# Alpha in 384 B rows, running sums in 64-row products, and more q, k turned by transfers, in a fused linear-attention and feed-forward kernel

## The chip, the cores and the metric

The kernel runs on one core of a Trainium2 chip. The metric is the device time of one execution in microseconds (us). The engines named are TensorE (PE, its weight loads PEld), VectorE (DVE), ScalarE (ACT), GpSimd (POOL) and SyncE (SP), which here only issues transfers (DMA).

## The reference

Attention with a decaying state, per batch and head, followed by a feed-forward stage on the same 3072 tokens of 384 features. B, H, S, D are 4, 8, 768, 48; d_ff is 768. All inputs and the output are float32.

```python
for t in range(S):
    state = alpha[:, :, t, :, None] * state + np.einsum('bhd,bhe->bhde', k[:, :, t], v[:, :, t])
    y[:, :, t] = np.einsum('bhd,bhde->bhe', q[:, :, t], state)
...
x = y.transpose(0, 2, 1, 3).reshape(B * S, H * D)
h = np.maximum(np.maximum(x @ w1, x @ w2), x @ w3)
out = h @ w_out
```

## The kernel before

The sequence is cut into 6 blocks of 128 tokens. A unit is one block of one batch with its 8 heads: 24 units, 0 to 23, batches inside blocks. Two units make a group, 12 in all. A group's alpha, q, k and v are loaded into tiles `an`, `qn`, `kn`, `vn` (five of each, in turn) with 128 tokens on the partitions and 16 heads of 48 float32 beside each other; a token's row of one head in DRAM is 192 B long. The first four groups are loaded by halves, one unit at a time, in an order written out by hand (`FIRST`), in which the pieces of the four weight matrices stand too ("w"; w1 is 0, w2 is 1, w3 is 2, w_out is 3, each cut after column 256 into piece 0 and piece 1).

Per group, ScalarE takes Ln of alpha into `la` (L538). Per unit, one product with a constant triangle (`tri`, L591, `cums`) gives the running sums of the logarithms, about the middle of the block. ScalarE makes exp of plus and minus that (`ep`, `en`, L594, L596). q times `ep` and k times `en` go to `qk` (L603, POOL or VectorE), v scaled to `v16` (L615 POOL, L610 ScalarE). Both q and k are then turned, so that features are on the partitions: by eight TensorE transposes and a VectorE copy (`turn_in`, L573, L577), or, for units in `CROSS_Q`, by one transfer from SP (`cross`, L622). Scores are eight products on 48 rows, in pairs on the upper and lower half of the array (L637); VectorE multiplies them with the causal mask into `LA` (L642); `LA` with v16, and the turned q with the state `Z`, give the output (L680, L683), which ScalarE scales into `xb` (L691). `xb` is turned into `xT` by three TensorE transposes and a copy (L705, L709) or, for units in `CROSS_X`, by a transfer (L697). The state of a block follows from the sums k times v (L735), VectorE (`U`, L741) and POOL (`Z`, L748), with factors `G` from the block's total decay (L551, L557, L563).

The feed-forward stage uses max(a, b, c) = a + relu(max(b - a, c - a)): `wd` holds w2 - w1 and w3 - w1 (L482, `subs`), and the term x @ w1 @ w_out is one product with `w1o`, made from w1 turned (L503, L509) and w_out (L520, `folded`). A feed-forward step (`ffn`) takes one unit (the first four) or two; per three or two columns blocks of 128 it multiplies with the w2 part (L776), ScalarE takes relu (L787), multiplies with the w3 part (L776), VectorE takes the maximum into `hT` (L792); then L810 multiplies with `w1o` and w_out, and the result leaves by ScalarE copies and transfers (L821, L829). w_out is loaded into the tile that w1 came in, once both pieces of w1 have been cast (L461).

The order of all instructions comes from a planner: each step has an engine, a cost in us, a rank, what it reads and writes, and the planner lists the steps of each engine by the time at which its own model has them ready; engines then work through their lists in order, and wait. `LEAD` ranks the feed-forward steps, `EARLY` names the engines of q, k, v work of some units, `SUBS` those of the differences, `PAIRS` the unit from which on two units' scores stand in one step. Loads keep the order of the program on SP; q, k transfers and xb transfers are put between them where the plan has them ready. `WARM` puts products with zeros (L717) on TensorE behind a unit's q or k product where the plan leaves TensorE free.

Of the kernel before, what the change touches and what calls it, by code (L numbers as in the profile page):

```python
# [10 lines left out]
FP32 = mybir.dt.float32  # L11
# [20 lines left out]
LEAD = (9.0, 7.5, 8.0, 9.0)  # L32
EARLY = {0: ("DVE", "DVE", "POOL"), 2: ("DVE", "POOL", "ACT"), 6: ("DVE", "POOL", "ACT"),
         8: ("DVE", "POOL", "ACT"), 11: ("POOL", "POOL", "ACT")}
WCUTS = (0, 256, 768)
SUBS = {(1, 0): "POOL", (1, 1): "DVE", (2, 0): "DVE", (2, 1): "POOL", (1, 2): "DVE",
        (2, 2): "POOL"}
FIRST = (("v", 1, 1, 2), ("va", 0, 1, 2), ("va", 0, 0, 1), ("k", 0, 1, 2), ("q", 1, 1, 2),
         ("a", 1, 0, 1), ("v", 1, 0, 1), ("k", 1, 0, 1), ("q", 1, 0, 1), ("k", 0, 0, 1),
         ("q", 0, 1, 2), ("w", 0, 0), ("a", 1, 1, 2), ("w", 0, 1), ("q", 0, 0, 1), ("w", 1, 1),  # L40
         ("k", 1, 1, 2), ("w", 3, 1), ("w", 3, 0), ("w", 1, 0), ("w", 2, 1), ("a", 2, 0, 1),
         ("w", 2, 0), ("k", 2, 0, 1), ("aq", 2, 1, 2), ("q", 2, 0, 1), ("q", 3, 0, 1),
         ("k", 2, 1, 2), ("a", 3, 0, 1), ("a", 3, 1, 2), ("v", 2, 0, 1), ("v", 2, 1, 2),
         ("k", 3, 0, 1), ("k", 3, 1, 2), ("q", 3, 1, 2), ("v", 3, 1, 2), ("v", 3, 0, 1))
WARM = (0, 1, 21)
WPOOL, ROWS, WTAX = {}, False, 0.1
SINGLE, LAST = 4, 0
PAIRS, WIDE = 10, 99
CROSS_Q = (18, 19, 20, 22, 23)
CROSS_X = (18, 19, 20, 21, 22, 23)  # L50
# [239 lines left out]
def kernel(  # L290
# [39 lines left out]
    halves = np.stack([rr < HALF, rr >= HALF], axis=1).astype(np.float32)  # L330
    c16_np = np.concatenate(
        [trimid, np.eye(P), (s_ <= t_).astype(np.float32), halves], axis=1
# [9 lines left out]
    c16 = sb.tile([P, 3 * P + 2], FP16, name="c16")  # L342
    c32 = sb.tile([P, 3], FP32, name="c32")
    tri, ident = c16[:, :P], c16[:, P:2 * P]
    maskA, hsel = c16[:, 2 * P:3 * P], c16[:, 3 * P:]
# [33 lines left out]
    w1o = sb.tile([P, NFT, DM], FP16, name="w1o")  # L379
    for t in las:  # L380
        nc.vector.memset(t[:, :, D:], 0.0)
    for t in qks:
        nc.vector.memset(t[:, :, :, D:], 0.0)
# [30 lines left out]
    def load(n, lo, hi, names="aqkv"):  # L414
        cb, g = divmod(n, B // UB)
        for x in names:
            t = ld[x][n % 5]

            def run(x=x, t=t):
                nc.sync.dma_start(  # L420
                    t[:, lo:hi],
                    views[x][cb * P:(cb + 1) * P, g * HG + lo:g * HG + hi])

            plan.step("SP", 0.5, -1.0, run, line="loads",
                      writes=[(x, n % 5, h) for h in range(lo // H, hi // H)],
                      load=1.80 * (hi - lo) / HG,
                      late=0.0 if n < 3 else SPARE)
            asked.append((x, n % 5, lo // H))
# [22 lines left out]
    def wload(g, part):  # L451
# [6 lines left out]
                  load=(3.15 if ROWS else 3.25) * size(part) / (NFT * DF) + WTAX)  # L458
# [19 lines left out]
    def subs(g, part):  # L478
# [7 lines left out]
                  reads=[("ws", g, part), ("w", 0, part)], writes=[("wd", g, part)])  # L486
# [44 lines left out]
    def decay(n):  # L531
        cb, g = divmod(n, B // UB)
        la, an = las[n % 3], ld["a"][n % 5]
        rank = 2 * n - 0.5

        def ln(lo, hi):
            plan.step("ACT", 0.2 + 0.00083 * (hi - lo) * D, rank,
                      lambda: nc.scalar.activation(out=la[:, lo:hi, :D], in_=an[:, lo:hi, :],  # L538
                                                   func=AFT.Ln, scale=1.0 / CDEC),
# [8 lines left out]
        def totals():  # L548
            live[key] = bank(key, [P, HG // 2, 2], FP32)
            for j in range(HG // 2):  # L550
                nc.tensor.matmul(live[key][:, j, :], la[:, 2 * j:2 * j + 2, :], hsel,  # L551
                                 start=True, stop=True)
# [14 lines left out]

    def turn_in(u, qk, qkT, tk):
        def trans():
            live[tk] = bank(tk, [P, 2, NP, P], FP16)  # L570
            for w in range(2):
                for j in range(NP):
# [3 lines left out]
                  reads=[("qk", u % 7, 0), ("qk", u % 7, 1)], writes=[tk, ("qkT room", u % 3)])  # L576
        plan.step("DVE", 0.69, u, lambda: nc.vector.tensor_copy(out=qkT, in_=live[tk]),  # L577
                  reads=[tk], writes=[("qkT", u % 3)])

    def prep(u):  # L580
# [3 lines left out]
        qk, v16 = qks[u % 7], v16s[u % 7]  # L584
        Lk, tk = ("Lp", u), ("tp", u)
        Ak = ("A", u)
        plan.width[Ak] = 2

        def cums():
            live[Lk] = bank(Lk, [P, H, D], FP32)  # L590
            nc.tensor.matmul(live[Lk], tri, la[:, hs, :D], start=True, stop=True)  # L591

        plan.step("PE", 0.162, u, cums, banks=[Lk], reads=[("la", n % 3, i)], writes=[Lk])
        plan.step("ACT", 0.49, u, lambda: nc.scalar.activation(out=ep, in_=live[Lk], func=AFT.Exp),  # L594
                  reads=[Lk], writes=[("ep", u % 3)])
        plan.step("ACT", 0.49, u, lambda: nc.scalar.activation(out=en, in_=live[Lk], func=AFT.Exp,  # L596
                                                               scale=-1.0),
                  reads=[Lk], writes=[("en", u % 3)])
        for w, x, e in ((0, "q", ep), (1, "k", en)):
            eng = EARLY[u][w] if u in EARLY else "POOL"  # L600
            plan.step(eng, 1.0 if eng == "POOL" else 0.56, u,
# [5 lines left out]
                      writes=[("qk", u % 7, w)])  # L607
# [11 lines left out]
        qkT, LA = qkTs[u % 3], LAs[u % 3]  # L619
# [5 lines left out]
        if u in CROSS_Q:  # L625
            plan.step("SP", 1.2, -2.0, cross, load=1.35, late=0.2,
                      reads=[("qk", u % 7, 0), ("qk", u % 7, 1)],
                      writes=[("qkT room", u % 3), ("qkT", u % 3)])
# [19 lines left out]
        if u < PAIRS:  # L648
            plan.step("PE", 0.23, u, scores, banks=[Ak], mode=1,
                      reads=[("qkT", u % 3), ("qkT room", u % 3)], writes=[Ak, ("LA room", u % 3)])  # L650
# [3 lines left out]
        else:  # L654
            first, made, v, Bk = held.pop()

            def both():
# [4 lines left out]
                      reads=[("qkT", x % 3) for x in (v, u)] + [("qkT room", x % 3) for x in (v, u)],  # L662
# [6 lines left out]
    def output(u):  # L669
        n, i = divmod(u, UB)  # L670
        cb, b = divmod(u, B)
        qkT, LA, v16, xb = qkTs[u % 3], LAs[u % 3], v16s[u % 7], xbs[u % 5]
# [262 lines left out]
```

## Time and profile before

| | |
|---|---|
| runs | 159.16, 157.71, 155.82 us; median 157.71 |
| profiled execution | 154.24 us, its span 152.5 us |
| TensorE busy | 133.9 us (88%), 1647 products |
| VectorE, ScalarE, POOL busy | 92.5, 87.2, 74.1 us |
| transfers | 30.58 MB, 114,211 packets, 107,792 of them under 512 B |
| SP's queue (q1) | 83.6% of 16 engines' span |
| granted TensorE clock | 0.996 of full |

The page cuts the span into 40 slices of 3.8 us and gives each engine's busy share of a slice in tenths, 9 for 90% or more; a busy TensorE can hold products that wait for nothing but their own pipeline. The chain of waits is followed back from the last instruction: at each step to what released it, or to the instruction ahead of it on its engine. In lists of instructions the bracket behind a line is the idle time of the engine before it and what ended it. The profiled execution is one execution on its own; the runs shown are others.

### The profile page before, as it was taken

What the parts mean: (1) busy time and instruction counts of PE and PEld (TensorE: products, weight loads), DVE (VectorE), ACT (ScalarE), POOL (GpSimd) and SP (SyncE); (2) the same over time, 40 slices, a digit from 0 to 9 for tenths busy, and PEclk for the clock granted to TensorE, in tenths of its full rate; (3) what the DMA queues carried; (4) which work ended last, traced back from release to release, by engine and by line L of the source; (5) the groups of instructions that cost most, each with busy time, mean ns of one, the idle gap of its engine ahead of it and who ended that gap; (6) DMA issues with size and microseconds to landing.
All of it is one profiled execution on the core that took longest, in us unless ns stands there. A gap on an engine that the chain in (4) does not pass through costs nothing.

```text
span 152.5 us, 4135 instructions
## 1 busy us (share of the span) xinstructions
PE 133.9 (88%) x1647; PEld 105.0 (69%) x1647; DVE 92.5 (61%) x159; ACT 87.2 (57%) x177; POOL 74.1 (49%) x101
## 2 busy tenths in 40 slices
PE   0133979999999999999999999999979999999990
PEld 0012567769789878698697888687867786868660
DVE  7004645837687998788595799484496583606030
ACT  3362476688367675687747667669419354543411
POOL 0423105184732619594987598598964880000000
PEclk9999999999999999999999999999999999999998
DMA  6999999989999989989899999989999976321113
GB/s 122 208 218 232 325 269 315 352 210 188 222 266 206 234 173 244 280 174 238 177 295 180 256 269 187 231 212 219 169 207 210 154 197 131 110 82 52 53 55 103
DMA packets 114211, 30.58 MB, mean 201 GB/s; under 512 B 107792, under 2 KB 113040, under 8 KB 114192
## 3 DMA queue, kind: packets, MB, share of 16 engines
q1 hardware_dynamic: 111744, 27.37, 83.6%
q10 hardware_dynamic: 2448, 2.95, 7.0%
q8 instruction: 13, 0.21, 0.5%
q14 instruction: 6, 0.05, 0.1%
HBM read 23.69 MB, written 4.72 MB: 186 GB/s over the span
## 4 chain that ended last, share of the span: by engine, by line
PE 76%; DMA 10%; SPq 8%; ACT 2%; issue 1%; POOL 1%; DVE 0%; ACTq 0%
PE psum L776 29%; PE psum L810 21%; SPq L420 7%; PE psum L573 5%; DMA ws<-in_moe_w_dram 4%; DMA qkT<-qk 4%; PE psum L637 4%; PE psum L683 3%; PE psum L591 2%; PE psum L680 2%; PE psum L705 2%; PE psum L717 2%; DMA xT<-xb 2%; PE psum L520 2%; PE psum L735 2%; PE psum L551 1%
## 5 line engine op out<-in xcount | busy, mean ns | idle before, releaser
L776 PE MATMUL psum<-xT,wd 128*128 128x256 f16 (+1 forms) x504 | 53.9, 257 | 0.3 <-DMA xT<-xb 0.2
L776 PEld LDWEIGHTS <-wd 128*128 128x128 f16 x504 | 42.0, 98 | 5.5 <-issue 0.5
L642 DVE TENSOR_TENSOR LA<-psum,c 128x1024 f16<-128x1024 f32 x24 | 28.6, 1220 | 9.7 <-PE psum L637 9.5
L792 DVE TENSOR_TENSOR hT<-psum,hT 128x512 f16<-128x512 f32 (+1 forms) x38 | 24.4, 659 | 16.1 <-PE psum L776 13.3
L787 ACT ACTIVATE hT<-psum 128x512 f16<-128x512 f32 (+1 forms) x38 | 21.7, 579 | 18.9 <-PE psum L776 18.3
L603 POOL TENSOR_TENSOR qk<-qn,ep 128x384 f16<-128x384 f32 x20 | 20.0, 1001 | 21.8 <-ACT ep L594 20.5
L603 POOL TENSOR_TENSOR qk<-kn,en 128x384 f16<-128x384 f32 x23 | 23.0, 1000 | 10.1 <-ACT en L596 8.7
L810 PE MATMUL psum<-wo,hT 128*128 128x384 f16 x144 | 27.3, 326 | 0.0
L810 PEld LDWEIGHTS <-hT 128*128 128x128 f16 x144 | 14.1, 98 | 9.3
L748 POOL TENSOR_TENSOR Z<-U,G 48x192 f16<-48x192 f32 x32 | 15.9, 504 | 7.4 <-DVE U L741 6.3
L691 ACT ACTIVATE xb<-psum,c 128x384 f16<-128x384 f32 x24 | 13.9, 581 | 8.6 <-PE psum L683 6.9
L591 PE MATMUL psum<-la,c 128*128 128x384 f16 x24 | 8.5, 352 | 9.7 <-ACT la L538 9.7
L577 DVE COPY qkT<-psum 128x1024 f16<-128x1024 f16 x19 | 12.9, 687 | 5.5 <-PE psum L573 4.6
L810 PE MATMUL psum<-w1o,xT 128*128 128x384 f16 x72 | 15.6, 326 | 0.0
L615 POOL TENSOR_SCALAR v<-vn,c 128x384 f16<-128x384 f32 x20 | 11.8, 588 | 6.7 <-DMA c<-const 3.8
L573 PE MATMUL psum<-c,qk 128*128 128x128 f16 x152 | 12.6, 234 | 2.7 <-DVE qk L603 2.7
L573 PEld LDWEIGHTS <-qk 128*128 128x128 f16 x152 | 10.4, 105 | 6.3 <-DVE qk L603 5.2
L538 ACT ACTIVATE la<-an 128x384 f16<-128x384 f32 (+1 forms) x16 | 10.9, 680 | 4.2 <-DMA an<-in_alpha_dram 3.4
L594 ACT ACTIVATE ep<-psum 128x384 f32<-128x384 f32 x24 | 11.9, 495 | 2.4 <-PE psum L591 1.8
L596 ACT ACTIVATE en<-psum 128x384 f32<-128x384 f32 x24 | 11.9, 498 | 0.0
L821 ACT COPY ob<-psum 128x384 f32<-128x384 f32 x14 | 6.7, 481 | 9.0 <-PE psum L810 8.9
L683 PE MATMUL psum<-v,LA 128*128 128x48 f16 x192 | 11.6, 186 | 0.0
(44 smaller groups left out, 152.5 us busy)
## 6 DMA issues: line engine op xcount, KB each, us to landing
an<-in_alpha_dram SPq DMA_DIRECT2D x8, 384.0 KB, 6.2
qn<-in_q_dram SPq DMA_DIRECT2D x8, 384.0 KB, 6.1
kn<-in_k_dram SPq DMA_DIRECT2D x8, 384.0 KB, 6.0
vn<-in_v_dram SPq DMA_DIRECT2D x8, 384.0 KB, 5.7
out_dram<-ob ACTq DMA_DIRECT2D x14, 192.0 KB, 3.9
ws<-in_moe_w_dram SPq DMA_DIRECT2D x3, 768.0 KB, 8.2
out_dram<-ob SPq DMA_DIRECT2D x9, 192.0 KB, 2.2
vn<-in_v_dram SPq DMA_DIRECT2D x8, 192.0 KB, 3.8
```

Source lines behind the costliest of these rows:

```text
L573: nc.tensor.transpose(live[tk][:, w, j, :], qk[:, w, 2 * j:2 * j + 2, :], ident)
L577: plan.step("DVE", 0.69, u, lambda: nc.vector.tensor_copy(out=qkT, in_=live[tk]), reads=[tk], writes=[("qkT", u % 3)])
L594: plan.step("ACT", 0.49, u, lambda: nc.scalar.activation(out=ep, in_=live[Lk], func=AFT.Exp), reads=[Lk], writes=[("ep", u % 3)])
L603: nc.gpsimd if eng == "POOL" else nc.vector).tensor_mul(
L642: lambda: nc.vector.tensor_mul(LA.rearrange("p a b t -> p (a b) t"), live[Ak].rearrange("p a (b t) -> p (a b) t", t=P), maskA.unsqueeze(1) ...
L683: nc.tensor.matmul(yp[:, 2 * j + p, :], LA[:, p, j, :], v16[:, 2 * j + p, :], start=(cb == 0), stop=True, skip_group_check=True)
L691: lambda: nc.scalar.activation(out=xb, in_=live[yk].rearrange("p a b -> p (a b)"), func=AFT.Copy, scale=ysc),
L748: eng.tensor_mul(Zn[rows, :, cols], U[rows, :, cols], G[rows, i * NP:(i + 1) * NP].unsqueeze(2).broadcast_to([D, NP, D]))
L776: nc.tensor.matmul(live[gk][:, jj, :], wd[:, kt, g, j * P:(j + 1) * P], xT[:, kt, :], start=(kt == 0), stop=(kt == NFT - 1))
L787: lambda h=h, gk=gk: nc.scalar.activation(out=h, in_=live[gk], func=AFT.Relu),
L792: lambda h=h, gk=gk: nc.vector.tensor_max(h, live[gk], h),
L810: nc.tensor.matmul(live[ok], a[:, i * P:(i + 1) * P], w, start=(kt == 0), stop=(kt == nk - 1))
```

## The change

- Alpha of groups 0 to 5 is loaded by unit with 64 partitions per unit, each partition holding two tokens in a row of 2 x 48 float32, 384 B (`SPLIT`, `turns`). Ln then writes two halves, even and odd tokens; the running sums are two products on 64 rows each, one for each parity (`tris`), and the totals take pairs of products with a new constant `hsel4`.
- For groups 2 to 5 (`TWINS`) the sums of both units stand in one step of four such products.
- q and k of units 12, 16, 19, 20, 21, 22, 23 are turned by transfers (before 18, 19, 20, 22, 23); xb of units 13, 20, 21, 22, 23 (before 18 to 23). Their sums, exp and products get an earlier rank (`AHEAD`).
- From unit 10 on four more `qk` tiles and four more `qkT` tiles are used, laid into the tiles that w3 and w2 came in (`MORE`, `ROOM`, `rotate`), with four POOL memsets (`clear`).
- Scores of two units stand in one step from unit 16 on (before 10). The order of the first loads, `LEAD`, `EARLY`, `SUBS` and `WARM` differ: 27 products with zeros instead of 21; w3's large difference on VectorE, w2's small one on POOL as before.

Counted in the built kernels: q, k transposes on TensorE 152 and 136; xb transposes 54 and 57; sums 24 products of 128 rows, and after it 12 of 128 rows and 24 of 64; SP transfers 11 and 12 that turn; alpha transfers of the first six groups 10 (192 B rows) and 12 (384 B rows).

```diff
-LEAD = (9.0, 7.5, 8.0, 9.0)
-EARLY = {0: ("DVE", "DVE", "POOL"), 2: ("DVE", "POOL", "ACT"), 6: ("DVE", "POOL", "ACT"),
-         8: ("DVE", "POOL", "ACT"), 11: ("POOL", "POOL", "ACT")}
+LEAD = (5.5, 6.5, 4.5, 6.5)
+EARLY = {0: ("POOL", "DVE", "POOL"), 1: ("POOL", "DVE", "POOL"), 3: ("POOL", "POOL", "POOL"),
+         4: ("DVE", "DVE", "ACT"), 5: ("POOL", "POOL", "POOL")}
-SUBS = {(1, 0): "POOL", (1, 1): "DVE", (2, 0): "DVE", (2, 1): "POOL", (1, 2): "DVE",
-        (2, 2): "POOL"}
+SUBS = {(1, 0): "POOL", (1, 1): "DVE", (2, 0): "DVE", (2, 1): "DVE", (1, 2): "DVE",
+        (2, 2): "DVE"}
...
+FIRST = (("v", 0, 1, 2), ("a", 1, 0, 1), ("a", 0, 1, 2), ("v", 1, 0, 1), ("k", 1, 0, 1),
+         ("a", 0, 0, 1), ("v", 1, 1, 2), ("w", 0, 1), ("v", 0, 0, 1), ("q", 1, 0, 1),
+         ("q", 0, 1, 2), ("q", 1, 1, 2), ("w", 0, 0), ("k", 0, 1, 2), ("a", 1, 1, 2),
+         ("qk", 0, 0, 1), ("w", 1, 0), ("k", 1, 1, 2), ("w", 1, 1), ("w", 3, 1), ("w", 3, 0),
+         ("k", 2, 0, 1), ("w", 2, 1), ("a", 2, 1, 2), ("w", 2, 0), ("a", 2, 0, 1),
...
-WARM = (0, 1, 21)
+WARM = (1, 0, 27)
-PAIRS, WIDE = 10, 99
-CROSS_Q = (18, 19, 20, 22, 23)
-CROSS_X = (18, 19, 20, 21, 22, 23)
+PAIRS, WIDE = 16, 99
+CROSS_Q = (12, 16, 19, 20, 21, 22, 23)
+CROSS_X = (13, 20, 21, 22, 23)
+AHEAD, ROOM, MORE = 5.0, 10, (4, 4)
+SPLIT, TWINS, ALOAD = 6, 2, 1.4
...
+    turns = [trimid[2 * at + r] for r in range(2)]
...
+            def turns(b, t=t):
+                nc.sync.dma_start(
+                    t[b * HALF:(b + 1) * HALF].rearrange("p (h r) d -> p h (r d)", r=2),
+                    alpha[g * UB + b, :, cb * P:(cb + 1) * P, :].rearrange(
+                        "h (p r) d -> p h (r d)", r=2))
...
+            if n < SPLIT:
+                rows = slice(lo // H * HALF, hi // H * HALF)
+                o = la[rows].rearrange("p (r h) d -> p h r d", r=2)[:, :, :, :D]
+                x = an[rows].rearrange("p (h r) d -> p h r d", r=2)
...
+            for r in range(2):
+                for x in us:
+                    key, rows = ("Lp", x), slice(x % UB * HALF, (x % UB + 1) * HALF)
+                    if r == 0:
+                        live[key] = bank(key, [P, H, D], FP32)
+                    nc.tensor.matmul(live[key], tris[r][rows], la[rows, r * H:(r + 1) * H, :D],
+                                     start=(r == 0), stop=(r == 1))
...
+    def rotate(first, more):
+        order, at = list(range(first)), []
+        for u in range(NU):
+            if u == ROOM:
+                order = list(range(first, first + more)) + order
+            at.append(order.pop(0))
+            order.append(at[-1])
+        return at
+
+    hq, ht = rotate(7, MORE[0]), rotate(3, MORE[1])
```

## The prediction

> **What bounds the kernel now.** I read the page's totals and slices first, then the chain of waits in order of time, then the timelines of TensorE and VectorE around the places that the chain names.
>
> ```profile
> PE 133.9 (88%) x1647; PEld 105.0 (69%) x1647; DVE 92.5 (61%) x159; ACT 87.2 (57%) x177; POOL 74.1 (49%) x101
> ...
> PE   0133979999999999999999999999979999999990
> ...
> DMA  6999999989999989989899999989999976321113
> ```
>
> Two resources are full at once. TensorE has no idle slice from about 22 us to the end, and the DMA engines are full from 2 us to about 118 us. The step that decides what an edit is worth is therefore where TensorE's full stretch begins, how much work it holds, and where it is interrupted.
>
> ```profile
> 13.63 6.50 DMA ws<-in_moe_w_dram
> 20.16 1.48 ACT w1h L461
> ...
> 25.55 0.33 PE psum L637 x8
> 25.88 1.73 PE psum L717 x10
> ...
> 28.94 1.18 PE psum L776 x18
> ...
> 106.31 5.70 DMA qkT<-qk
> 112.05 0.40 PE psum L637 x8
> ...
> 120.14 3.11 DMA xT<-xb
> ```
>
> This is the chain (start, us, what). Up to 28.94 us TensorE waits on data: line 717, the products with zeros, fills it. At 28.94 the first product of the feed-forward stage (L776) starts, and from there to its last product at 148.8 TensorE is back to back. Going through its starts one by one, I find only two holes over 0.1 us: 1.12 us before 112.05 (a q, k transfer) and 0.40 us before 123.39 (an xT transfer). So span = start of the first L776 + work + 1.6 of holes + 3.7 after the last product.
>
> What released 28.94 is VectorE (start, us, engine, line, what):
>
> ```profile
> 25.99 1.23 DVE L642 TENSOR_TENSOR LA<-psum,c 128x1024 f16<-128x1024 f32 x1 [0.64 <-PE psum L637]
> 27.14 1.75 DVE L482 TENSOR_TENSOR wd<-ws,w1h 128x1536 f16<-128x1536 f32 x1
> ```
>
> The large piece of w2 had landed at 23.00, but its difference (L482) stood behind the mask product of unit 0, which hung on that unit's q, k, the last of them (q) landed at 20.98.
>
> **Part 1, DMA.** In 4 to 12 us the queue carries only 192 B rows:
>
> ```profile
> q1 hardware_dynamic: 9061, 1.71, 109.8%
> ```
>
> That is 8 us x 16 x 1.098 / 9061 = 15.5 ns a packet, so a unit's load (1024 packets over 16 engines) is 0.99 us. The packet records give 38 ns for 768 B, 90 ns for 2048 B. No row has 384 B. On the straight line between 192 and 768 B it is 23 ns; then an alpha unit (512 packets) takes 0.73 us and saves 0.25. The bounds: a packet that costs as much as one of 192 B (saves 0.49), or twice that (saves 0). I take 0.25, since 768 B costs far under four times 192 B. Twelve units save 3.0 us of DMA, 1.0 of it in the first four.
>
> [...]
>
> The new order puts w1 first and moves w2's small piece ahead of its large one. Up to w2's large piece after has one unit more (+0.99), the small piece (384 packets of 1024 B at 52 ns = 1.24), a constant 64 KB larger (+0.17), and alpha's -1.0: +1.3 on 23.00, so it lands at about 24.3. Unit 0's k lands at 20.98 - 1.0 + 0.17 = 20.1. A hole goes: SP stood from 17.2 to 21.7 before the load of w_out, which shares w1's tile and waited for w1's casts; w_out then landed 4.12 us after the piece before it, for 2.4 of packets. With w1 cast by 17 that 1.7 us is gone.
>
> **Part 2, the start.** The first product of the stage needs the difference of w2 and unit 0's xT, both on VectorE. In the new order VectorE runs: k of unit 0 (20.1 + 0.56), TensorE's transposes and the score product of unit 1, its mask product (to about 22.0), qkT of unit 0 (0.69), scores, mask product (1.23, to about 24.5), xT 0.36, the large difference 1.75 (24.85 to 26.6), xT 0.36: 26.9. Ends: 26.4, if qkT and scores follow at once; 27.7, if the seven zero products placed between unit 1's output and unit 0's scores run at the slow clock (0.32 each, as in 14 to 24 us, instead of 0.162). I take 26.9: 2.0 us earlier than 28.94. The alpha Ln on 64 partitions is longer (0.84 for 768 elements against 0.52) and four units need two products each, but q and k land later than both, which covers it; without that cover it would add 0.3 to 0.6. Moving w3's large difference from POOL (3.10) to VectorE (1.75) lets the second half of the stage start by 33 instead of 35; TensorE has 6 us of fold and first-half work there.
>
> **Part 3, TensorE's work after that point**, each from start to start of the next. Transposes of q, k (L573): 152 to 136, 16 x 56 ns = -0.90. Transposes of xb: +3 x 56 = +0.17. The sums of groups 2 to 5: two 162 ns products become four on 64 rows, run two by two; the trace shows no such product of 384 columns, but the score products on 48 rows do run in pairs (second start 4 ns after the first, a pair every 56 ns), so 2 x 162 again: 0. Bounds: 0, and 4 groups x 0.324 = 1.3 if they do not pair. Entering and leaving split rows costs 96 + 93 ns (product-to-score start 205 instead of 109, score-to-next 148 instead of 55). From the first L776 on, before does this 12 times (units from 10 on have scores in pairs), after 17 times: pairs begin at unit 16 and one group's sums stand alone. +0.95. Sum: +0.2.
>
> [...]
>
> **Part 4, the transfers of q, k.** Before has five, all after 103 us; after has seven: units 12 and 16 stand among the loads of SP's queue. One costs 1024 packets at 18 to 25 ns, 1.2 to 1.6 us; by landings, 108.57 - 107.03 = 1.54, and the next one 3.44 (108.57 to 112.01) as SP held it until its product was there. Queued behind each: the next group's loads, whose alpha feeds Ln, the sums, then POOL. Ahead of the last alpha there are three such transfers and an xT instead of two transfers, so its landing is 114.34 - 3.0 + 0.2 - 1.7 + 1.5 + 0.5, about 112; 110 if none waits as the second did. TensorE comes to that group's sums with 31.8 us of work left, at 26.9 + 117.8 - 31.8 = 112.9. So loads and TensorE stay level, 0 to 2 us apart. The transfers are issued further ahead of their use, so I take the 1.12 hole as gone and 0.8 in all for holes instead of 1.6. Bounds 0 and 3. The other engines: POOL loses a difference of 3.1 and gains a product of 1.0, three v of 0.59 and four memsets, which have no row on POOL (between 0.1, its smallest, and 0.59 each). With four products, two v and four Z updates it needs 7.2 us a group, against 8.2 of loads (59.33 to 100.15 for five groups), so it stays covered; without that cover qk and then TensorE would be late by the excess. VectorE gains 1.75 and 0.35 and loses two copies of 0.69 and a product of 0.6; ScalarE gains eight times 0.31 on Ln and loses three v of 0.61: both under 70% busy, nothing on the path.
>
> **Sum:** -2.0 (start) + 0.2 (work) - 0.8 (holes) = -2.6. The profiled execution has a span of 152.5 and a time of 154.24, so after 149.9 and 151.6. The three runs have a median of 157.71, 3.5 above the profiled one; I take the saving off the median: 155.1.
>
> **Rivals.**
> (a) The start gains nothing: slow-clock zeros and VectorE's order put the first product at 28.9. Speaking for it: before's own difference stood 4 us after its data. Against: unit 0's k is earlier, and w2 has its place by then. -2.6 + 2.0 = -0.6: 157.1.
> (b) 384 B rows save nothing. The first product slips 1.0; the last alpha lands 3.0 later, at 113 to 115, and its sums wait 1 to 2. -2.6 + 1.0 + 1.2: 157.3. Part 1's straight line speaks against it; no row decides it.
> (c) The slower one: SP's queue. A q, k transfer waits at the head of SP for POOL's product, and the loads behind it stand still. The second transfer of before shows it: 3.44 instead of 1.54. Three before the last alpha at 3.44 are +5.7, TensorE stands about 4.8: 155.1 + 4.8 = 159.9. It beats the gain from (2.6 + 0.9 of slack) / 3 = 1.2 extra each, so from 2.7 us a transfer. Against it: TensorE reaches unit 12's sums at 26.9 + 117.8 - 76.6 = 68.1, four POOL products later its q, k are there at about 73, and SP comes to the transfer when the loads of the group after it are issued, at about 71; a wait of 2 us is covered by what is already queued, since a load lands 6 us (median) after its issue.
> (d) More than forecast: first product at 25.5 and no hole: -1.4 - 0.8, 152.9.
>
> **How the numbers follow.** Forecast 0.43, (a) 0.13, (b) 0.12, (c) 0.17, (d) 0.15. A measurement here can tell about 2% from no change, 3.2 us: faster is below 154.6, slower above 160.9. The forecast lies 0.6 inside "same"; its own range, from the ends of the start and of the holes, is 153.8 to 156.7, and some 0.45 of it falls below 154.6. That is 0.20; with (d) and 0.01 of the runs' spread in (a) and (b), 0.36. Of (c), 0.10 has transfers long enough to pass 160.9 (4 us each and more); 0.04 is for what no row shows. Same 0.50. The range for 8 in 10 is 151.8 to 159.8: below, (d) less a us of spread; above, (c) at its shown price.
>
> **What would show it.** Right: first product of the stage at 26 to 27.7; no slice under 9 on TensorE from there; alpha loads of 192 KB in 512 packets of 22 to 24 ns; 17 entries into split rows; holes under 1 us. Wrong: packets of 30 ns; a gap on SP ahead of the transfers for units 12, 16 or 19 and, behind it, TensorE waiting for alpha or for qkT between 70 and 125 us; the four-product sums lasting 0.65 us.

## The result, and the profile after

The changed kernel takes 161.8 us (median of four runs, 159.76 to 164.37) against 158.0 for the kernel before on the same chip: a ratio of 1.035, 95% interval 1.025 to 1.045, some 5.5 us slower. The medians hold slow executions too, and the ratios and intervals, here and below, are of the undisturbed ones alone, so a ratio is not the quotient of the medians. The profiled execution took 161.9 us with a span of 160.1.

The totals, TensorE's slices, the granted clock and the DMA slices of the kernel after (each slice is 4 us here):

```profile
PE 137.2 (86%) x1652; PEld 103.3 (65%) x1652; DVE 92.1 (58%) x158; ACT 88.5 (55%) x174; POOL 74.7 (47%) x108
...
PE   0234789797999999999997999899959999999990
...
PEclk9999999999999999999999999999996999999999
DMA  5999999998999999998997998999979995341112
```

TensorE's row now has slices of 7, 8 and 5 from 20 us to 120 us, where before, from 23 us on, had a single 7. One slice of the clock row is a 6. The DMA engines are full until about 132 us instead of 118.

The chain of waits in order of time (start, us, what) says why. Before, it ran nearly all through TensorE from 28.94 us on and left it for two transfers; now it keeps leaving TensorE for a load:

```profile
27.96 9.72 DMA ws<-in_moe_w_dram
37.70 0.97 DVE wd L516
38.72 0.68 PE psum L851 x9
...
59.13 3.93 DMA an<-in_alpha_dram
63.14 0.85 ACT la L587
64.03 0.50 PE psum L660 x4
...
82.77 2.08 PE psum L851 x18
...
112.09 6.75 DMA ws<-qk
118.83 0.04 issue
118.88 0.40 PE psum L712 x8
119.28 3.74 PE psum L851 x18
```

The last weights, alpha, and unit 19's q, k in turn release TensorE. The last two lines of L851 are the same eighteen products as the line at 82.77, in 3.74 us instead of 2.08: the clock, granted at 0.50 from 119.39 to 122.80 us.

VectorE's difference of w2's large piece, and TensorE's timeline at the start of the feed-forward stage (start, us, engine, line, what; in brackets the idle time and what ended it):

```profile
27.62 1.76 DVE L516 TENSOR_TENSOR wd<-ws,w1h 128x1536 f16<-128x1536 f32 x1 [0.63 <-DMA ws<-in_moe_w_dram]
```
```profile
28.02 0.50 PE L851 MATMUL psum<-xT,wd 128*128 128x128 f16 x6
29.43 1.43 PE L851 MATMUL psum<-xT,wd 128*128 128x128 f16 x21 [0.92 <-DVE wd L516]
...
36.55 1.68 PE L851 MATMUL psum<-xT,wd 128*128 128x128 f16 x27 [0.45 <-DVE wd L516]
```

The first product comes 0.9 us earlier than before (28.02 against 28.94), but only the six that need w2's small piece, whose difference POOL had ended at 24.40. Behind them TensorE stands for 1.08 us, counted from start to start less the product's own time, and the products that need the large piece, as before's did at 28.94, come at 29.43. VectorE had waited 0.63 us for that piece, which landed at 27.60.

The whole, from first product to last, made of the starts of TensorE's products: the last product ends 7.68 us later (156.49 against 148.81) although the first starts 0.92 earlier. Holes are 7.97 us in all (1.08, 0.62, 0.64, 0.20 up to 39 us; 0.19, 0.43, 0.20, 0.48 up to 80; 1.11 at 86.7, 0.89 at 99.9, 2.13 at 116.7) against 1.53 before: +6.44. The halved clock behind the last hole costs 3.74 - 2.08 = 1.66. What is left, 7.68 + 0.92 - 6.44 - 1.66 = 0.50, is work.

### The profile page after: what moved, and what is told of

It is laid out like the page before. It is cut to its first block, busy times and chain, and to the rows that moved or that the text cites. A ratio compares the mean times of both kernels' runs of the same rounds, so it can differ in the third digit from the quotient of the medians.

```text
span 160.1 us, 4146 instructions
## 1 busy us (share of the span) xinstructions
PE 137.2 (86%) x1652; PEld 103.3 (65%) x1652; DVE 92.1 (58%) x158; ACT 88.5 (55%) x174; POOL 74.7 (47%) x108
## 4 chain that ended last, share of the span: by engine, by line
PE 33%; DMA 32%; SPq 20%; issue 4%; ACT 3%; DVE 3%; POOL 3%; ACTq 0%; POOLq 0%
PE psum L851 15%; DMA an<-in_alpha_dram 12%; PE psum L885 11%; SPq L449 11%; DMA vn<-in_v_dram 8%; DMA ws<-in_moe_w_dram 6%; SPq L443 5%; DMA ws<-qk 4%; SPq L487 4%; DMA out_dram<-ob 2%; ACT la L587 2%; POOL v L690 1%; PE psum L712 1%; PE psum L758 1%; POOL Z L823 1%
## 5 line engine op out<-in xcount | busy, mean ns | idle before, releaser
L851 PE MATMUL psum<-xT,wd 128*128 128x256 f16 (+1 forms) x504 | 55.9, 262 | 1.9 <-DVE wd L516 1.9
L851 PEld LDWEIGHTS <-wd 128*128 128x128 f16 x504 | 42.3, 99 | 9.1 <-DVE wd L516 2.6
L862 ACT ACTIVATE hT<-psum 128x512 f16<-128x512 f32 (+1 forms) x38 | 21.4, 574 | 10.4 <-PE psum L851 9.7
L587 ACT ACTIVATE la<-an 64x768 f16<-64x768 f32 (+1 forms) x16 | 13.5, 842 | 24.1 <-DMA an<-in_alpha_dram 23.6
L678 POOL TENSOR_TENSOR qk<-qn,ep 128x384 f16<-128x384 f32 x16 | 16.0, 1005 | 14.4 <-ACT ep L669 7.8
L690 POOL TENSOR_SCALAR v<-vn,c 128x384 f16<-128x384 f32 x23 | 13.4, 588 | 17.2 <-DMA vn<-in_v_dram 12.3
L637 DVE COPY qkT<-psum 128x1024 f16<-128x1024 f16 x12 | 8.1, 686 | 13.9 <-PE psum L632 13.3
L885 PE MATMUL psum<-w1o,xT 128*128 128x384 f16 x72 | 15.6, 326 | 0.0
L678 POOL TENSOR_TENSOR qk<-kn,en 128x384 f16<-128x384 f32 x14 | 13.9, 998 | 0.9 <-DMA kn<-in_k_dram 0.9
L660 PE MATMUL psum<-la,c 64*128 64x384 f16 x24 | 4.9, 368 | 9.2 <-ACT la L587 9.2
L816 DVE TENSOR_TENSOR U<-psum,Z 128x384 f32<-128x384 f32 x16 | 8.5, 550 | 4.2 <-PE psum L810 4.2
L758 PEld LDWEIGHTS <-LA 128*128 128x128 f16 x192 | 9.6, 96 | 0.8 <-DVE LA L717 0.2
L904 ACT COPY ob<-psum 128x384 f32<-128x384 f32 x9 | 4.3, 483 | 10.3 <-PE psum L885 9.5
```

Source lines behind the costliest of these rows:

```text
L587: lambda: nc.scalar.activation(out=o, in_=x, func=AFT.Ln, scale=1.0 / CDEC),
L678: nc.gpsimd if eng == "POOL" else nc.vector).tensor_mul(
L690: lambda: nc.gpsimd.tensor_scalar(out=v16, in0=ld["v"][n % 5][:, hs], scalar1=vsc, scalar2=1.0, op0=AOP.mult, op1=AOP.mult),
L758: nc.tensor.matmul(yp[:, 2 * j + p, :], LA[:, p, j, :], v16[:, 2 * j + p, :], start=(cb == 0), stop=True, skip_group_check=True)
L851: nc.tensor.matmul(live[gk][:, jj, :], wd[:, kt, g, j * P:(j + 1) * P], xT[:, kt, :], start=(kt == 0), stop=(kt == NFT - 1))
L862: lambda h=h, gk=gk: nc.scalar.activation(out=h, in_=live[gk], func=AFT.Relu),
```

## The experiments

The theories. T1, named theory A in the first four expectations: what costs is that alpha is received by 64 partitions, not its 384 B rows. T2: the q, k transfers among the loads cost more than their packets. The rivals: the rows themselves, the new order of the first loads, and the planner's new lists as a whole.

### Rows and partitions

**Loads alone.** A kernel that only loads alpha, in six phases of ten units of 192 KB, one queue, with zeros as output: 192 B rows on 128 partitions; 384 B on partitions 0 to 63; 384 B on the two halves in turn; 384 B on 128 partitions; 192 B on 64 partitions by two transfers; the second kind mixed with k.

```diff
+ for load in (rows192, half384, turns384, wide384, half192, mixed):
+     for i in range(10): load(i)
```

> Not the computation: it leaves everything out except loads of alpha and k from SP, in six phases of ten unit loads (192 KB each) with a barrier between phases, and writes zeros. Phase 1: 192 B rows on 128 partitions. 2: 384 B rows, all on partitions 0 to 63. 3: 384 B rows, lower and upper 64 partitions in turn. 4: 384 B rows on 128 partitions (token pairs of 256 tokens, half the heads). 5: 192 B rows on 64 partitions (two transfers a unit). 6: phase 3 in turn with phase 1. Theory A (a transfer that ends on 64 partitions is slower for it, whatever its rows): a unit takes about 0.9 to 1.0 us in phase 1, 1.0 or more in 2, 1.0 to 1.2 in 3, 0.7 in 4, 1.2 or more in 5. Theory B (384 B rows are slow as such): phase 4 is as slow as phase 3, and phase 5 as fast as phase 1. Theory C (neither; alpha's rows are not what costs): 0.7 in phases 2, 3, 4 and 1.0 in 1 and 5.

The queue's line for 36 to 44 us (384 B on 64 partitions), 57 to 63 us (halves in turn) and 75 to 81 us (384 B on 128); the columns are packets, MB and the share of 16 engines:

```profile
q1 hardware_dynamic: 3990, 1.48, 123.4%
...
q1 hardware_dynamic: 3775, 1.40, 124.2%
...
q1 hardware_dynamic: 4325, 1.61, 101.1%
```

Read as in the prediction: 8 x 16 x 1.234 / 3990 = 39.6 ns a packet, 6 x 16 x 1.242 / 3775 = 31.6 ns, 6 x 16 x 1.011 / 4325 = 22.4 ns. The row is the same; the partitions make it 22 or 40. By landings a unit takes 1.06, 0.85 and 0.73 us (the last five of the 128 kind 0.60), and 0.79 for the 192 B rows (the last four, clear of the output's writes). So 384 B rows save on 128 partitions, but not where the change puts them: on the lower 64 a unit is dearer than it was, and with the halves in turn, which is nearer to what the change does, it saves nothing (0.85; 0.89 a unit when mixed with loads of k). Theory A had 1.0 to 1.2 for the halves in turn, which was too much. The phase of 192 B on 64 partitions was limited by issuing (1.36 us a unit) and shows nothing.

The phases of 384 B rows on the lower 64 and on 128 partitions moved 185 and 268 GB/s (1.48 MB in 8 us, 1.61 in 6): half the partitions are the slower side, by 1.45 here. What makes them slower, these runs do not show.

**In the kernel, the order kept.** Three kernels keep the planner's order of after, instruction by instruction, and change alpha's loads and sums alone.

```diff
 e1: alpha of groups 0 to 5 in 192 B rows on 128 partitions, sums of 128 rows, as before
-    t[b * HALF:(b + 1) * HALF].rearrange("p (h r) d -> p h (r d)", r=2),
-    alpha[g * UB + b, :, cb * P:(cb + 1) * P, :].rearrange("h (p r) d -> p h (r d)", r=2))
+    t[:, b * H:(b + 1) * H],
+    views["a"][cb * P:(cb + 1) * P, g * HG + b * H:g * HG + (b + 1) * H])
 e2: as e1, but 384 B rows on 128 partitions: other alpha values than the reference's
+    alpha[g * UB + b, :NP, cb * P:(cb + 2) * P, :].rearrange("h (p r) d -> p h (r d)", r=2))
 e3: as after (64 partitions, 64-row sums), each unit by two transfers of 192 B rows
+    for r in range(2): ...rearrange("h (p r) d -> p h r d", r=2)[:, :, r])
```

> The changed kernel with its planned order unchanged, but alpha of the first six groups loaded and used as before: 192 B rows on 128 partitions, one sum product of 128 rows a unit. Theory A (the 64-partition alpha loads hold up the queue): w2's large piece lands near 24 instead of 27.6, the last load near 115 instead of 130, the holes at 28 and 38 us go, and the time falls from 161.8 to 153 to 156. Theory B (the queue is held up by the q, k transfers and their waits): the first 80 us get at most 1 us faster and the holes at 87, 100 and 117 us stay: 159 to 161. Theory C (the order of the first loads is at fault): w2's large piece still lands at 27, first product of the feed-forward stage near 28, 158 to 161.

Measured 155.9 us, ratio 1.021 (1.011 to 1.031), against 1.035 (1.025 to 1.045) of after: inside theory A's range, though the intervals overlap. The signs came only in part: w2's large piece landed at 26.11 instead of 27.60 (theory A had 24), the last load at 126.8 instead of 129.9 (theory A had 115), the hole at 38 us went, and the one at 28 (1.18) and unit 19's (1.57) stayed.

> As the kernel with 192 B rows, in the same planned order, but alpha of the first six groups comes in 384 B rows on all 128 partitions: token pairs of two blocks, half the heads, so the values in the alpha tile are others than the reference's, at equal work. Theory A (64 partitions are the cost, 384 B rows are cheap): as fast as the 192 B version or 1 to 2 us faster. Theory B (384 B rows are slow as such): as slow as the changed kernel, 160 to 162.

Measured 153.7 us, ratio 1.003 (0.997 to 1.009): 1.8% or 2.7 us under e1, by the rows alone. Its packets of 384 B took 24.9 ns on the mean, median 22, and the last of these loads landed at 57.32 instead of 60.14.

> The changed kernel with each alpha load of the first six groups made by two transfers of 192 B rows onto the same 64 partitions. Theory A (64 partitions are the cost): as slow as the changed kernel or slower by up to 3 us. Theory B (384 B rows are the cost): back to 154 to 157.

Measured 160.2 us, ratio 1.049 (1.023 to 1.074): with 192 B rows on 64 partitions it is as slow as after. These are two runs with a wide interval, and the kernel differs from e1 in more than the receiving partitions: it issues each of these alpha loads as two, and Ln and the sums work on 64 rows, as in after. Its 192 B packets took 16.1 ns up to 62 us, hardly more than e1's 15.5. So it speaks against the rows as the cost, but does not show by itself that the receiving side is. What Ln and the sums on 64 partitions cost apart from the loads, no run tells. T1 rests on the kernel that only loads, on e2 (the rows are a gain), and on the two pairs that differ in the partitions: the next run, and one under the transfers from ScalarE's queue.

**The split alone.** The kernel before with SPLIT and TWINS, all else as before.

```diff
+SPLIT, TWINS, ALOAD = 6, 2, 1.4
```

> The kernel before, its order of loads, its transfers, its engines; only alpha of the first six groups comes in 384 B rows on 64 partitions, with 64-row sums. T1 (64 partitions at the receiving end are the main loss, 1.06 instead of 0.81 us a unit and slower neighbours): last alpha lands 4 to 6 us later than the 114 us of before, time 4 to 6 us over before (ratio 1.025 to 1.04). Rival (it costs only together with the new transfers and order): within 1.5 us of before (ratio under 1.01).

Measured 158.0 us, ratio 1.028 (1.020 to 1.035): +4.2 us, in the range of T1. Its sign came only in part: the last split load landed 4.3 us late (63.58, before 59.33), but the last alpha of all at 111.33, 3.0 us early and not 4 to 6 late. The loss is ahead of that: holes of 3.7 us between 28 and 65 us, where before had none. The queue from 4 to 12 us, where before had 9061 packets at 109.8%:

```profile
q1 hardware_dynamic: 7057, 1.62, 132.6%
```

Less is moved (1.62 MB instead of 1.71) in more of the engines' time. The packet records say where: in these 8 us the 384 B packets took 34.2 ns, and the 192 B packets of q, k and v beside them 21.4 instead of 15.6. So the loss isn't alpha's only; what is in flight with it is slowed too.

### The start alone

The kernel before with FIRST, WARM, LEAD, EARLY and SUBS of after.

> The kernel before with only the new first loads, zero products, ranks and engines (FIRST, WARM, LEAD, EARLY, SUBS); 192 B rows, transfers of before. T2: the first product of the feed-forward stage at 26 to 27 us instead of 28.9 and nothing lost later, 2 us under before (ratio 0.985 to 0.99). Rival (what the start gains is lost again on the weights' differences and on holes later): ratio 1.00 or over.

Measured 155.6 us, ratio 1.005 (1.000 to 1.009): the rival. The first product came at 27.85, 1.1 us earlier, the first behind the large difference at 28.44, and holes of 0.25, 0.37, 0.96, 0.23 and 0.16 us followed up to 36 us; the gain is gone.

### The transfers

**The set of transfers alone, and taken back.** f4 is the kernel before with after's CROSS_Q, CROSS_X, AHEAD and MORE (its pairs of scores stand from unit 10, not 16 as the expectation has it); f1 is after with 192 B rows and before's CROSS_Q and CROSS_X.

```diff
 f4: -CROSS_Q = (18, 19, 20, 22, 23)
     +CROSS_Q = (12, 16, 19, 20, 21, 22, 23)
     +AHEAD, ROOM, MORE = 5.0, 10, (4, 4)
 f1: the reverse of the first two lines, on after with SPLIT = 0
```

> The kernel before with only the new set of transfers (q, k of seven units, xb of five), their earlier ranks, the additional tiles and pairs of scores from unit 16; 192 B rows, first loads of before. T2: TensorE waits for the transfers of units 12 and 19 some 0.5 to 1.5 us each and on what they push back, 1 to 3 us over before (ratio 1.006 to 1.02). Rival (the transposes saved come through): 0.5 to 1 us under before (ratio 0.994 to 0.997).

Measured 157.1 us, ratio 1.019 (1.009 to 1.029): +2.9 us, as T2 said. TensorE's timeline shows two of the waits:

```profile
84.39 0.62 PE L711 MATMUL psum<-ws 48*128 48x128 f16 x16 [0.88 <-DMA ws<-ws]
...
98.92 0.40 PE L711 MATMUL psum<-qkT 48*128 48x128 f16 x8 [1.42 <-DMA qkT<-qk]
```

But holes of 0.6, 1.0 and 0.3 us stand at 34 to 51 us too, ahead of any transfer: the planner's lists had changed there as well.

> The changed kernel with alpha in 192 B rows on 128 partitions throughout and with the q, k and xb transfers of the kernel before (units 18, 19, 20, 22, 23 and 18 to 23). Beside the run with 192 B rows in after's order (e1, 155.9 us) only the transfers differ. T2 (a q, k transfer stands behind the loads and lands some 10 us after its product is there): the holes ahead of units 12 and 16 go, TensorE gets the sixteen transposes back (+0.9), 153 to 154.5 us. Rival (the new order of the first loads is what eats its own gain): 155.5 to 156.5 as with the transfers.

Measured 155.4 us, ratio 1.014 (1.006 to 1.022), between the two. Its profile has a 1.2 us hole at 25.5 and one of 0.96 at 28.3 and then the clock at half for 6.8 us, and only 1.0 us of holes after 36 us; so the time can't decide, and the trace speaks for T2.

**The same transfers from ScalarE's queue.** Nothing moves but the engine that issues the q, k transfers.

```diff
-            nc.sync.dma_start_transpose(out=qkT...
+            nc.scalar.dma_start_transpose(out=qkT...
```

> The kernel before, its five q, k transfers issued by ScalarE. T2: the second transfer's 5.7 us from issue to landing (106.3 to 112.0) falls to about 3 and the hole of 1.12 us goes: 0.5 to 1.1 us under before, ratio 0.993 to 0.997. Rival (ScalarE stands in front of POOL's product instead): ratio 1.00 to 1.01.

Measured 159.0 us, ratio 1.032 (1.026 to 1.039). The rival, and dearer than it said. ScalarE's and TensorE's timelines:

```profile
125.29 0.48 ACT L829 COPY ob<-psum 128x384 f32<-128x384 f32 x1 [5.63 <-POOL v L615]
```
```profile
125.82 1.44 PE L776 MATMUL psum<-xT,wd 128*128 128x256 f16 x6 [3.72 <-ACT ob L829]
```

ScalarE stood 5.6 us with the transfer at its head; the copy behind it holds a bank that TensorE wants. It did not stand for POOL, as the rival had it and the bracket has it: the last of POOL's four products there ended at 122.85, while ScalarE's waits ahead of the transfer ended at 123.37 and 123.85, when two xb transfers that SP had issued landed. Why the program waits for these, the record doesn't say.

> The kernel of the run with the new transfers alone (157.1 us, last alpha landed at 114.5), every q, k transfer issued by ScalarE in a queue of its own instead of by SP behind the loads; nothing else moves. T2 (the loss is the stay behind the loads: issued at 79.2 and landed at 84.4, issued at 113.1 and landed at 118.7): landing 2 to 3 us after the product on POOL, the holes ahead of units 12, 16 and 19 (1.0, 1.1, 1.6) gone, 153.5 to 155 us, ratio 0.995 to 1.008. Rival (transposing packets cost the DMA engines the same wherever they are issued, and ScalarE now waits for POOL in SP's place): 156.5 to 158.5, ratio 1.017 to 1.03, with ScalarE idle 1 us or more ahead of the issues.

Measured 161.7 us, ratio 1.053 (1.044 to 1.062). 

> The run with alpha in 192 B rows in after's planned order (155.9 us, u19's transfer issued at 107.9 and landed at 113.9, 1.57 of hole behind it), every q, k transfer issued by ScalarE. T2: u19's lands by 108, that hole and the 0.37 of unit 12 go, 153.5 to 154.5 us. Rival: 155.5 to 157.

Measured 156.5 us, ratio 1.018 (1.012 to 1.025), as e1. 

> The changed kernel, its seven q, k transfers issued by ScalarE; alpha still on 64 partitions. T1 and T2 together: the holes of 1.11 (unit 12) and 2.13 (unit 19) and the halved clock after the second go, but the loads still come 5 us late: 157 to 159.5 us, ratio 1.018 to 1.03. Rival: as after, 161 to 163, ratio 1.03 to 1.05.

Measured 159.7 us, ratio 1.037 (1.029 to 1.046), as after. This kernel and the one ahead of it differ in alpha's loads and sums alone, and their intervals are apart: 1.9% or 2.9 us for alpha on 64 partitions.

In all four the transfers still landed 3 to 8 us after their issue, 4 to 6 in most. A queue of its own does not shorten that: the part of T2 that blamed the place in SP's queue fell.

**Parts of the set.** Three more with the plan rebuilt, on f4 or before:

```diff
 j2: f4, CROSS_Q = (19, 20, 21, 22, 23)
 j3: f4, AHEAD = 0.0
 j4: before, PAIRS = 16
 k:  before, CROSS_Q = (20, 22, 23)
```

> The run with the new transfers alone (157.1 us, ratio 1.019; its pairs of scores stand from unit 10 as in the kernel before), with the q, k of units 12 and 16 turned by TensorE again. T2b (a transfer among the loads lands 4 to 6 us after its issue, TensorE's way takes about 2): the holes of 0.9 (84.4) and 1.4 us (98.9) go, the sixteen transposes cost 0.9, loads come 1.5 to 3 us earlier: 154.5 to 155.5, ratio 1.004 to 1.011. Rival (ranks and tiles, not the transfers, move other work late): 156.5 to 157.5, ratio 1.016 to 1.024.

Measured 159.5 us, ratio 1.033 (1.026 to 1.039): neither theory's. The holes ahead of units 12 and 16 went, and others came:

```profile
97.36 0.48 PE L652 MATMUL psum<-la,c 128*128 128x384 f16 x2 [0.94 <-ACT la L586]
...
107.35 0.32 PE L652 MATMUL psum<-la,c 128*128 128x384 f16 x1 [1.30 <-ACT la L586]
```

> The run with the new transfers alone, without the earlier ranks of the sums, exp and products of units 12, 16 and 19 to 23 (AHEAD 0). T2b: the products come later and the transfers with them, the holes ahead of units 12, 16, 19 grow by 0.5 to 1 us each: 157.5 to 160, ratio 1.022 to 1.04. Rival (the ranks are the cost): 154.5 to 156, ratio 1.004 to 1.015.

Measured 160.4 us, ratio 1.042 (1.032 to 1.052): the earlier ranks are a help, as T2 had it; without them TensorE waits 1.2 us for unit 19's transfer and 1.5 for a later one.

> The kernel before with scores in pairs from unit 16 instead of unit 10, nothing else. Both theories: three groups more enter split rows twice, 3 entries at 0.19 are 0.6 us of TensorE, ratio 1.002 to 1.006; what waits two units for a pair comes earlier, which can give some back.

Measured 157.5 us, ratio 1.018 (1.010 to 1.025), 2.7 us instead of 0.6. The profile shows holes of 0.93 for POOL's q, k and 0.70 for a transfer of xb and a first product at 30.47. The late start is not the edit's: this kernel has before's instructions in before's order up to 71 us on every engine. So have, up to 36 us at least, the kernels k, f4, j2, j3 and the first one issued by ScalarE, and their first products came at 27.63, 26.89, 28.07, 28.23 and 30.07, before's at 28.94. A start read from one trace is therefore good to some 2 us only. What makes up the rest of the 2.7 us stays open.

> The kernel before with the q, k of units 18 and 19 turned by TensorE (transfers of units 20, 22, 23 only). T2b: the hole of 1.12 us at 110.9 goes, sixteen transposes add 0.9, the last loads come 1.5 to 3 us earlier, so 1 us under to no change, ratio 0.993 to 1.000. Rival: 0.9 us over, ratio 1.004 to 1.008.

Measured 154.6 us, ratio 0.999 (0.994 to 1.003): two transfers fewer and sixteen transposes more come to the same, inside T2's range. No version of the whole computation beats the kernel before.

**The transfers left out, the order kept.** Since each new set re-lists all engines, the last two runs keep after's order and leave the transfers of units 12, 16 and 19 out, once with 192 B rows, once as in after.

```diff
         def cross():
+            if u in (12, 16, 19): return
...
-        qkT = qkTs[ht[u]]
+        qkT = still if u in (12, 16, 19) else qkTs[ht[u]]
```

> The run with alpha in 192 B rows in after's planned order (155.9 us, ratio 1.021), order unchanged, with the q, k transfers of units 12, 16 and 19 left out: their scores and outputs read a constant tile, so these values are others, and TensorE waits for none of the three. If the transfers are the second cause: holes of 0.37 and 1.57 go, the last alpha lands 3 to 4 us earlier than 116.2, 152.5 to 154 us, ratio 0.995 to 1.008. Rival (the planned order is, holes elsewhere stay): 155 to 156.5, ratio 1.013 to 1.023.

Measured 154.0 us, ratio 1.005 (0.999 to 1.011), against 1.021 (1.011 to 1.031) with them: 1.6%, 2.5 us for three transfers, with intervals that just touch.

> The changed kernel, order unchanged, with the same three transfers left out (the values of these units are others). If they are the second cause: holes of 1.11 (86.7) and 2.13 (116.7) and the halved clock behind the second (1.7) go, loads land 3 to 4 us earlier from 90 us on: 156.5 to 158.5, ratio 1.018 to 1.03. Rival: with alpha this late TensorE waits for the sums or for POOL's products instead: 160 to 162, ratio 1.04 to 1.05.

Measured 156.0 us, ratio 1.026 (1.010 to 1.043). By the time alone this can't be told from after's 1.035, since the intervals overlap; the profiled execution has a span of 152.3, and TensorE's row has one slice under 9 after 31 us:

```profile
PE   0243889899999999999989999999999999999990
```

The loads show it most plainly. From unit 12's group on, after's alpha lands every 10.4 us (79.53, 90.15, 99.97, 110.55, 121.04); without the three transfers every 8.4 (76.87, 85.64, 95.09, 102.71, 110.45). That is (41.5 - 33.6) / 3 = 2.6 us a transfer; with 192 B rows it is (40.0 - 33.9) / 3 = 2.0. The packet records give the same: the 1024 packets of 256 B of units 12, 16 and 19 took 22.6, 42.8 and 52.3 ns on the mean, over 16 engines 1.45, 2.74 and 3.34 us, or 2.5 a transfer. In e1 they took 22.6, 23.5 and 49.9 ns: 1.45, 1.50 and 3.19 us, or 2.0 a transfer. So the loads behind come later by what the packets themselves take of the engines. Most take 18 ns, a few far longer. Unit 19's transfer, in DMA slices of 0.15 us from 114 to 120 us of the kernel after:

```profile
DMA  9999999999999817000000001999999999999999
GB/s 207 211 201 256 289 251 336 327 413 284 261 181 97 26 25 17 9 9 10 17 31 20 22 17 29 270 285 316 418 389 410 235 259 259 259 264 264 259 259 264
```

For 1.8 us (115.95 to 117.75) the engines move 9 to 31 GB/s. They are not free then: a packet's time is booked in the slice in which it starts, and the zeros are engines held by packets that began earlier. Of this transfer 18 packets started from 115.52 to 116.31, and all of them ended between 117.74 and 117.77, the longest after 2.25 us. Half of the others start before (115.0 to 116.3) and half after (117.3 to 118.3). Unit 16's transfer has 20 such packets, which ended together at 104.60 to 104.63; unit 12's has none. A packet of 16 KB of the queue q8 (instructions) ran beside them both times (115.20 to 116.14, 102.63 to 103.74), and beside unit 19's in e1, where 22 packets ended together (111.20 to 112.16); there was none beside unit 12's. Whether that is what holds them, no run tells.

## Why the prediction was wrong

**Forecast 155.1, range up to 159.8; measured 161.8.** The bound it named, two resources full at once, was right, and so was its consequence that late loads reach TensorE. Three terms of its sum failed, all of them about transfers: the price of alpha's rows, the start, and the price of the q, k transfers. The account below compares single traces in places, and these scatter, so the sizes are good to a us or two.

**Part 1, the price of a 384 B packet.** The straight line gave 23 ns, and rows of 384 B do take 22 to 25 ns: on 128 partitions (e2, 2.7 us under e1, where part 1 had 3.0 us of transfer time). The change puts them on 64, where they took 32 (halves in turn) to 40 ns (lower half) by themselves, 30.2 on the mean in after and 34.2 at the start of f2, around and over the upper bound of 31, and slowed the rows beside them (21.4 ns instead of 15.6 in f2). Part 1 asked what a row costs by its length and never where it lands; neither the saving of 0.25 a unit nor the bound of 0 held, it was a loss (2.2 to 3.3 us of the kernel's time with the order kept). The trace of before could not show it, since every load there fills 128 partitions. Rival (b) priced the rows at no saving; it was short for the same reason.

**Part 1 and part 2, the start.** w2's large piece landed at 27.60, not 24.3; in the same order it came at 26.1 in e1 and in the last run, so executions differ by 1.5 us here and none reaches the forecast. Part 2 made its sum up to the products behind the large difference, and put VectorE's order in their way. They came at 29.43 (27.95 in e1, 27.90 in the last run), not at 26.9, and what they waited for in after was the landing: VectorE stood ready for 0.63 us. With before's first loads the same products came between 26.89 and 30.47, so no gain of the start shows. More than the size, the step that failed is that the start was taken as one wait: three differences of weights stand behind the first six products, and each that is late reopens the hole (1.08, 0.62 and 0.64 us). f3 shows the same without the split. Rival (a), a start that gains nothing, is what happened: f3 is 0.5% over before.

**Part 3, TensorE's work,** was right: +0.2 forecast, +0.5 left over. Entering and leaving split rows took 96 + 92 ns, and the four sums ran in pairs (starts at 64.032, 64.038, 64.194 and 64.211 us):

```profile
64.03 0.50 PE L660 MATMUL psum<-la,c 64*128 64x384 f16 x4 [0.27 <-ACT la L587]
```

But j4, the later start of the pairs by itself, cost 2.7 us, so the entries' 0.19 may not be all that such a change of the plan moves.

**Part 4, the transfers of q, k.** This is the term that was mis-sized: the price of 1.5 us each, 18 to 25 ns a packet, was 2.0 to 2.6, up to 52 ns a packet, and the last alpha landed at 121.04 instead of 112. The hole of 1.12 us did not go; it was replaced by 1.11 (unit 12) and 2.13 (unit 19), and one of 0.89 for a product of POOL. The prediction took these transfers as issued further ahead of their use. But a transfer among loads takes 5.5 to 6.7 us from issue to landing, where TensorE's own way takes 0.45 us of transposes and a copy of 0.69, and SP came to unit 12's at 82.12, not at about 71. SP's issues of units 12, 16 and 19:

```profile
82.12 3.65 SPq L697 DMA_TRANSPOSE ws<-ws  x1
...
100.04 2.74 SPq L697 DMA_TRANSPOSE qkT<-qk  x1
...
112.09 3.05 SPq L697 DMA_TRANSPOSE ws<-qk  x1
```

**Rival (c)** was the nearest, with 159.9 and 0.17, but in part by luck. That the transfers hold back the loads behind them is there. That SP waits at its head for POOL's product is not: the four products of unit 12's group had ended by 79.67, unit 16's by 97.02 and the four of unit 19's group by 108.23, 2.4 to 3.9 us before SP came to the transfers. SP's rows of 2.7 to 3.7 us are as long as those of some loads there (up to 3.0), and 1.25 at 121.89 and 124.40 in before, behind its last load. The row that (c) was read from says the same: the second transfer of before was issued at 106.31 in 1.24 us, its group's products had ended by 103.73, and its packets ran until 111.42, so its 3.44 us were not SP's wait. The wait of 2 us that the prediction held covered did not arise. The price of 3.44 was too much a transfer, and the split supplied the remainder.

**How the parts add up.** With the order kept, in ratios to before: 1.005 with neither the 64 partitions nor the three transfers, 1.021 with the transfers, 1.035 with both. So some 0.8 us are the order, 2.5 the transfers and 2.2 the partitions; taken the other way round the partitions are 3.3 and the transfers 1.4, all with some 1.5 us of uncertainty; by the pair issued by ScalarE the partitions are 2.9. The start, alone on before, costs the same 0.5% as the order. On before the split costs 4.2 and the transfers 2.9, more than inside the change. And what the plan's lists are worth by themselves stays open: j2 and j4 moved the time by some 2% with a single constant, and no run here takes that apart.

## What to carry to other kernels

A transfer has two sides: before a longer row is bought by laying data on fewer partitions, price the receiving side by a kernel that only loads (39.6 ns a packet on 64 partitions here, 22.4 on 128). Where queue and TensorE are both full, an operation moved from TensorE to a transfer is paid at the price of the full queue, here 2 to 2.6 us of all later loads for 0.45 us of transposes, and its landing decides whether it is in time. Add up the packets' times, not only their number: a few that are held can double the price (3.34 us for unit 19's 1024 packets, 1.45 for unit 12's). To size one step of a kernel whose order a planner makes, keep the order and leave the step out; a rebuilt plan measures the plan.

## What the runs showed of the hardware that was not expected

The hole of 2.13 us ahead of unit 19's scores cost 1.66 us more than its length. The windows of the kernel after around unit 19's transfer (us, busy time and number of instructions by engine, then the granted clock, the DMA share and GB/s):

```profile
116.00:119.00 3.00, 1.03 (x18) 0.62 (x17) 1.29 (x2) 1.16 (x2) 2.92 (x5) 1.00 0.62 144
119.00:122.80 3.80, 3.80 (x26) 2.63 (x23) 2.59 (x4) 0.84 (x1) 1.35 (x3) 0.55 1.18 224
122.80:126.00 3.20, 3.20 (x45) 2.50 (x44) 0.96 (x2) 2.45 (x6) 0.81 (x1) 1.00 1.06 180
```

After 2.13 us without a product the clock records show half speed from 119.39 to 122.80 us, 3.41 us, while TensorE works without a pause; that is the 1.66 us above. Not every execution has it: three of the four runs of after have a mean clock of 0.989 or 0.990, the shortest (159.76 us) one of 1.000. In f1 holes of 1.2, 0.4 and 0.96 us between 25 and 29.3 us went with 6.8 us at half speed:

```profile
28.80:35.60 6.80, 6.33 (x53) 4.82 (x54) 4.61 (x7) 4.39 (x8) 0.00 (x0) 0.50 1.05 288
```

In the 3.41 us ahead of the slow stretch TensorE was busy for 1.44 us in after and for 1.80 in f1, so it was not idle throughout. Single holes of 1.5 to 1.6 us (e1, f4, j3) were followed by no slow stretch. What sets a slow stretch off, these runs do not show.
